# Reordering the opening of an FFT-plus-SoLU kernel: the zeroing of a table, a load of indices, and two small weight products

## The chip, the cores and the metric

The kernel runs on one core of one Trainium2 chip. Its time is the device time of one execution in microseconds (us). Before the change three runs gave 1119.38, 1119.64 and 1119.69 us, a median of 1119.64 us. The profile is one execution with the hardware profiler on.

The engines go by short names: PE is TensorE (its weight loads are PEld), DVE is VectorE, ACT is ScalarE, POOL is GpSimd, and SP is SyncE, which here only issues transfers. Lines are numbered as in the kernel before; L644 is its line 644.

## The reference

```
x: (8, 3136, 256)      w_in: (256, 1024)   w_out: (1024, 256)   g_ln: (1024)
X   = real(fft over axis 1, then fft over axis 2)          # the mixing block
x   = X.reshape(25088, 256)
h   = x @ w_in
sm  = softmax(h, axis=-1)
s   = h * sm                                                # SoLU
ln  = (s - mean(s)) / sqrt(var(s) + 1e-6) * g_ln
out = ln @ w_out
```

In this setup w_in and w_out are 64-bit floats in memory and are narrowed to 32 bits by integer and float operations on DVE and ACT.

## The kernel before, in words

The transform over the sequence (3136 = 49 x 64) is done in two steps, for pairs of batches (four pairs). Step one, `transform1`, multiplies slabs of x by the table F. Step two, `transform2`, multiplies the stored result by the table T. The transform over the features is not done on the data: it is folded into w_in once, at the start. `product_in(h, parts)` multiplies the cosine table Q into w_in and gives the folded matrix Wi, one half h of 128 rows at a time. Each half h has four parts: parts 0 and 2 read the upper half of w_in (c = 0), parts 1 and 3 the lower half (c = 1); parts 0 and 1 make the left 512 columns, parts 2 and 3 the right 512. `keep_in` copies the finished half from PSUM to Wi on ACT.

After the opening the kernel goes through 100 units of 128 or 256 rows each. In each, PE makes the rows' second transform and the up product, DVE and ACT make the softmax and the statistics, and PE makes the down product. The change does not touch this loop.

The order of instructions on each engine is written out by hand (`with tc.manual_schedule()`), so an engine executes in the order of the source, and a waiting instruction holds everything behind it on the same engine. The opening, which the change rearranges, consists of these pieces:

- **Loads.** SP issues, in order: the row indices `idx` (L806), the four pieces of w_in (`raw_in`, L591, 512 KB each), Q (L674), F (L818), and then the slabs of x. A slab c of the first pair (c = 0 to 7, four positions each) has two operands: `xa` or one half of `room`, read straight by SP (L128), and `xb` or the other half of `room`, its mirror image, gathered by POOL with an indirect DMA that needs `idx` (L130). The first six slabs are asked for at once, the last two when slabs 0 and 1 have been used. `gain` is g_ln in 8 rows of 128 (L678).
- **Narrowing of w_in**, piece by piece (0, 1: upper half left and right; 2, 3: lower half left and right). `exponent_in` takes the exponent bits (L594, DVE) and has ACT scale them in three steps (`confine`, L618, L620, L622). `narrow_in` then takes the mantissa (L594, then L635, its part 0), joins sign and exponent (L638, part 1, waits for ACT), and multiplies (L644, part 2).
- **Products.** `busy` runs four matmuls whose result is not used (L703). Then `product_in` (L698): before the change parts 0 and 2 of both halves, then parts 1 and 3 of half 0; parts 1 and 3 of half 1 come only behind slab 4.
- **First transform.** For each slab DVE adds the mirror image (`add_mirror`, L146, L148). Slabs 0 and 2 then go to PE directly (L214, four matmuls for each two positions); the others are first folded on DVE (`fold`, L153, L154, L166) into one of two `y` buffers and need two matmuls for each two positions (L225). ACT copies each result out (L228), and SP stores it to `zd` in DRAM (L233). Four PSUM banks are used in turn.
- **The norm weights.** `scale_out` transposes `gain` on PE (L722) into the PSUM bank that slab 3 uses next, and ACT scales it into `g_ln` (L723), which the narrowing of w_out needs. It stands behind slab 2.
- **The table T.** POOL zeroes it (two memsets, L829) behind the six gathers; SP fills its two diagonal blocks later (L683).
- **The end of the opening.** w_out is loaded after slab 3's turn (L717) and narrowed on DVE; `zd` is read back (L241), the second transform of the first units starts, and DVE meets the first unit at L302.

Of the kernel before, what the change touches and what calls it, by code (L numbers as in the profile page):

```python
# [45 lines left out]
def kernel(  # L46
# [19 lines left out]
    nc = tc.nc  # L66
# [3 lines left out]
    KD = D // P  # L70
# [21 lines left out]
    T = [const.tile([P, 2, n, N2], FP32, name=f"T{n}") for n in (KG, NK - KG)]  # L92
# [6 lines left out]
    idx = const.tile([P, NP * (NC + NK)], I32, name="idx")  # L99
# [19 lines left out]
    def load(pr, c, room=None):  # L119

        r = slice(pr.p * PR, (pr.p + 1) * PR)
        rows = PR if pr.p else P
        if room is None:
            xa = xpool.tile([P, CH, D], FP32, tag="xa", name="xa")
            xb = xpool.tile([P, CH, D], FP32, tag="xb", name="xb")
        else:
            xa, xb = (t.rearrange("p (l d) -> p l d", d=D) for t in room)
        nc.sync.dma_start(out=xa[0:rows], in_=x_pn[r.start : r.start + rows, c * CH + 1 : (c + 1) * CH + 1, :])  # L128
        i = pr.p * NC + c
        nc.gpsimd.indirect_dma_start(  # L130
            out=xb[0:rows].rearrange("p l d -> p (l d)"), out_offset=None, in_=x_g,
            in_offset=bass.IndirectOffsetOnAxis(ap=idx[0:rows, i : i + 1], axis=0))
        xa, xb = xa[0:PR], xb[0:PR]
        x0 = None
        if c == NC - 1:
            x0 = xpool.tile([PR, 1, D], FP32, tag="x0", name="x0", bufs=1)
            nc.sync.dma_start(out=x0, in_=x_pn[r, 0:1, :])
        pr.raw[c] = (xa, xb, x0)

    def add_mirror(pr, c, engine, part=None):  # L140

        xa, xb, _ = pr.raw[c]
        rows = (0, CH) if part is None else (part * CH // 2, (part + 1) * CH // 2)
        r = slice(rows[0], min(rows[1], CH - 1 if c == NC - 1 else CH))
        a, rb = xa[:, r, :], xb[:, ::-1, :][:, r, :]
        i = engine.tensor_tensor(out=a[:, :, 1:D], in0=a[:, :, 1:D], in1=rb[:, :, D - 1 : 0 : -1], op=ALU.add)  # L146
        if part is None:
            engine.tensor_tensor(out=a[:, :, 0:1], in0=a[:, :, 0:1], in1=rb[:, :, 0:1], op=ALU.add)  # L148
        return i
# [6 lines left out]
    def fold(pr, c):  # L156

        xa, _, x0 = pr.raw.pop(c)
        pr.y[c] = xpool.tile([PR, CH, D], FP32, tag="y", name="y")
        sides = [(pr.y[c], xa)]  # L160
        if c == NC - 1:
            pr.y0 = xpool.tile([PR, 1, D], FP32, tag="y0", name="y0", bufs=1)
            sides.append((pr.y0, x0))
        for o, i in sides:
            fold_features(o, i)
            nc.vector.tensor_copy(out=o[:, :, 0:129:128], in_=i[:, :, 0:129:128])  # L166
# [426 lines left out]
    def bits(o, i, a, op0, b=None, op1=ALU.bypass):  # L593
        nc.vector.tensor_scalar(out=o, in0=i, scalar1=a, scalar2=b, op0=op0, op1=op1)  # L594
# [11 lines left out]
    def confine(unit, here=False, parts=(0, 1, 2)):  # L606

        if unit is None:
            return
        if here:  # L610
            bits(unit, unit, -896.0, ALU.add, 0.0, ALU.max)
            bits(unit, unit, 255.0, ALU.min, 2.0 ** 23, ALU.mult)
            return

        u = unit.bitcast(FP32)
        for i in parts:
            if i == 0:
                nc.scalar.activation(out=u, in_=unit, func=ACT.Relu, bias=limits[:, 0:1])  # L618
            elif i == 1:
                nc.scalar.activation(out=u, in_=u, func=ACT.Relu, bias=limits[:, 1:2], scale=-1.0)  # L620
            else:
                nc.scalar.activation(out=unit, in_=u, func=ACT.Identity, bias=limits[:, 2:3], scale=-(2.0 ** 23))  # L622

    def narrow(w, raw, outs, unit, parts=range(3)):

        if w.dtype == FP32:
            if 2 in parts:
                for o, scale in outs:
                    nc.vector.tensor_scalar(out=o, in0=o, scalar1=scale, scalar2=2.0 ** 20, op0=ALU.mult, op1=ALU.mult)
            return  # L630
        lo, hi = raw[:, 0 : 2 * NW : 2], raw[:, 1 : 2 * NW : 2]
        m = lo.bitcast(FP32)
        if 0 in parts:
            bits(mantissa, hi, 0xFFFFF, ALU.bitwise_and, 0x100000, ALU.bitwise_or)
            nc.vector.scalar_tensor_tensor(out=m, in0=lo.bitcast(U32), scalar=2.0 ** -32, in1=mantissa, op0=ALU.mult,  # L635
                                           op1=ALU.add)
        if 1 in parts:
            nc.vector.scalar_tensor_tensor(out=unit, in0=hi, scalar=top_bit, in1=unit, op0=ALU.bitwise_and,  # L638
                                           op1=ALU.bitwise_or)
        if 2 in parts:  # L640
            n = NW // len(outs)
            for i, (o, scale) in enumerate(outs):
                r = slice(i * n, (i + 1) * n)
                nc.vector.scalar_tensor_tensor(out=o, in0=m[:, r], scalar=scale, in1=unit[:, r].bitcast(FP32),  # L644
                                               op0=ALU.mult, op1=ALU.mult)

    class Weights:
# [17 lines left out]
            self.units.append(exponent(w, raw))  # L665
            confine(self.units[-1])

        def narrow_in(self, i):
            w, raw, o, c, j, n = self.pieces[i]
            narrow(w, raw, [(o[:, j : j + n], 2.0 ** -19)], self.units.pop(0))  # L670

        def load_tables(self):
            self.Q = fpool.tile([P, KD, D + 1], FP32, tag="ev", name="Q", bufs=1)
# [129 lines left out]
    with tc.manual_schedule():  # L803
        pairs = [Pair(p) for p in range(NP)]
        first, weights = pairs[0], Weights()
        nc.sync.dma_start(out=idx, in_=mirror)  # L806
        make_identity(nc, ident)

        rooms = {}
        for c in range(2, 6, 2):  # L810
# [4 lines left out]
        for c in range(4):  # L815
            weights.piece_in(c)
        weights.load_tables()
        nc.sync.dma_start(out=F, in_=f_tab)  # L818
        for c in range(6):
            load(first, c, rooms.get(c))  # L820
            if c == 0:
                weights.load_gain()
        nc.vector.memset(ones, 1.0)
        nc.vector.memset(neg_half, -0.5)
        bits(top_bit, neg_half[:, 0:1].bitcast(I32), 31, ALU.logical_shift_right, 31, ALU.logical_shift_left)
        for i, limit in enumerate((-896.0, 255.0, 255.0 * 2.0 ** 23, 1e-12)):
            nc.vector.memset(limits[:, i : i + 1], limit)
        for t in T:
            nc.gpsimd.memset(t, 0.0)  # L829
        weights.exponent_in(0)  # L830
        for c in range(3):
            weights.exponent_in(c + 1)
            weights.narrow_in(c)
        weights.narrow_in(3)
        weights.mid()
        first.minus = fpool.tile([P, D], FP32, tag="ot1", name="minus", bufs=3)[0:PR, 0:ZR]
        nc.scalar.mul(out=first.minus, in_=F[:, 1, :], mul=-1.0)
        weights.busy(3, 4)
        made = [weights.product_in(h, (0, 2)) for h in range(KD)]
        weights.keep_in(0, weights.product_in(0, (1, 3), made[0]))  # L840
        for c in range(NC):

            add_mirror(first, c, nc.vector)
            if c not in BY_PE:
                fold(first, c)
            if c == NC - 1:
                for i in range(2):
                    weights.exponent_out(i)
                confine(weights.units[0], True)
                weights.narrow_out(0)  # L850
            if c == 3:
                weights.place_out()
                for i in range(2):
                    weights.load_out(i)
                weights.load_table(0)
                weights.scale_out()
            for s in range(CH // 2):
                if c == NC - 1:
                    confine(weights.units[0], parts=(s,))
                transform1(first, c * CH // 2 + s)  # L860
            first.raw.pop(c, None)
            if c + 6 < NC:
                load(first, c + 6)
            if c == 4:
                weights.keep_in(1, weights.product_in(1, (1, 3), made[1]))

        turn(first, 0, nc.sync, 0, 2)
        turn(first, 0, nc.gpsimd, 2, KG)
# [131 lines left out]
        for i in range(whole + 1, len(units) + lag + 1):  # L1000
# [84 lines left out]
            if i in (len(units), len(units) + 1):  # L1085
                w = i - len(units)
# [89 lines left out]
```

## Time and profile before

| what | value |
|---|---|
| median of three runs | 1119.64 us |
| the profiled execution's own time | 1119.93 us |
| its span, first to last instruction | 1117.8 us |
| PE busy | 1095.0 us (98%) |
| DVE busy | 976.6 us (87%) |
| ACT busy | 798.9 us (71%) |
| POOL busy | 809.2 us (72%) |
| first unit met by DVE (L302) | 52.76 us from the span's start |

The span leaves out 2.1 us that the execution's own time has around it. In a timeline line the first number is the start in us from the span's start, the second the time from the first to the last of the x instructions that the line merges, and a bracket at its end gives the idle time of that engine just before and what ended it. A name with "q" (SPq, POOLq) is the queue in which an engine issues transfers. In the forty slices a digit is the busy share of a slice of 27.9 us in tenths.

### The profile page before, as it was taken

What the parts mean: (1) busy time and instruction counts of PE and PEld (TensorE: products, weight loads), DVE (VectorE), ACT (ScalarE), POOL (GpSimd) and SP (SyncE); (2) the same over time, 40 slices, a digit from 0 to 9 for tenths busy, and PEclk for the clock granted to TensorE, in tenths of its full rate; (3) what the DMA queues carried; (4) which work ended last, traced back from release to release, by engine and by line L of the source; (5) the groups of instructions that cost most, each with busy time, mean ns of one, the idle gap of its engine ahead of it and who ended that gap; (6) DMA issues with size and microseconds to landing.
All of it is one profiled execution on the core that took longest, in us unless ns stands there. A gap on an engine that the chain in (4) does not pass through costs nothing. (4 is left out here: it accounts for less than half of the span.)

```text
span 1117.8 us, 22047 instructions
## 1 busy us (share of the span) xinstructions
PE 1095.0 (98%) x7055; PEld 875.5 (78%) x7055; DVE 976.6 (87%) x1432; ACT 798.9 (71%) x1947; POOL 809.2 (72%) x709
## 2 busy tenths in 40 slices
PE   5999999999999999999999999999999999999998
PEld 3557787878877878787788788787887788778888
DVE  7999888888888988889889989898898898998884
ACT  4598777777766777777766777777776777777771
POOL 4077888857867979775876878885775676866674
PEclk9999999999999999999999999999999999999999
DMA  9565887766978989766897888776696685865665
GB/s 347 195 186 123 180 205 181 177 144 142 181 175 171 198 180 199 178 147 141 154 182 171 189 184 196 183 176 149 138 165 141 138 172 114 164 140 114 141 133 125
DMA packets 457930, 187.75 MB, mean 168 GB/s; under 512 B 424646, under 2 KB 439254, under 8 KB 457816
## 3 DMA queue, kind: packets, MB, share of 16 engines
q1 hardware_dynamic: 443800, 146.94, 61.9%
q0 software_dynamic: 14016, 39.40, 13.1%
q8 instruction: 57, 0.93, 0.3%
q14 instruction: 57, 0.47, 0.1%
HBM read 46.75 MB, written 38.80 MB: 77 GB/s over the span
## 5 line engine op out<-in xcount | busy, mean ns | idle before, releaser
L289 PE MATMUL ps_h<-Wi,q 128*128 128x512 f32 x800 | 361.6, 593 | 0.3 <-DVE nmax L310 0.2
L465 POOL TENSOR_TENSOR S<-uT 128x512 f32<-128x512 f32 x186 | 237.5, 1277 | 107.6 <-DVE u L325 29.4
L472 PE MATMUL ps_m<-Ws,S 128*128 128x128 f32 x2304 | 296.0, 275 | 0.1
L472 PEld LDWEIGHTS ps_m<-Ws,S 128*128 128x128 f32 x2304 | 279.5, 192 | 3.2 <-issue 0.2
L332 ACT ACTIVATE h<-u,usum 128x1024 f32<-128x1024 f32 x196 | 224.9, 1148 | 71.5 <-DVE u L325 71.5
L289 PEld LDWEIGHTS ps_h<-Wi,q 128*128 128x128 f32 x800 | 144.2, 190 | 144.9 <-issue 141.9
L325 DVE SCALAR_TENSOR_TENSOR u<-h,u 128x1024 f32<-128x1024 f32 x196 | 232.8, 1223 | 11.0 <-ACT u L318 10.9
L318 ACT ACTIVATE u<-h,nmax 128x1024 f32<-128x1024 f32 x196 | 223.2, 1141 | 2.3 <-DVE nmax L310 1.1
L396 DVE STREAM_TRANSPOSE v<-u 128x2048 f32<-128x2048 f32 x88 | 203.4, 2311 | 3.0
L472 PE MATMUL ps_m<-Wo,uT 128*128 128x128 f32 x1536 | 203.7, 276 | 0.4 <-DMA out_dram<-ot 0.4
L472 PEld LDWEIGHTS ps_m<-Wo,uT 128*128 128x128 f32 x1536 | 187.9, 192 | 1.5 <-issue 1.5
L310 DVE CUSTOM_DVE_ANT_0 h<-ev,ps_h 128x1024 f32<-128x1024 f32 x100 | 122.1, 1221 | 17.1 <-DVE ev L302 9.3
L559 POOL DMA_INDIRECT out_dram<-ot,idx x96 | 110.5, 1151 | 29.0 <-issue 12.4
L310 DVE CUSTOM_DVE_ANT_0 h<-h,ps_h 128x1024 f32<-128x1024 f32 x96 | 117.2, 1221 | 14.2 <-ACT ot L516 0.5
L465 POOL TENSOR_TENSOR S<-uT,S 128x512 f32<-128x512 f32 x93 | 118.9, 1278 | 7.2
L465 POOL TENSOR_TENSOR S<-S,uT 128x512 f32<-128x512 f32 x93 | 118.8, 1277 | 7.3
L302 DVE SCALAR_TENSOR_TENSOR ev<-w_mid,r,ps_h 128x1024 f32<-128x1024 f32 x99 | 122.8, 1241 | 0.2
L472 PE MATMUL ps_m<-Ws,uT 128*128 128x128 f32 x768 | 101.8, 276 | 0.0
L472 PE MATMUL ps_m<-Wo,S 128*128 128x128 f32 x768 | 101.4, 275 | 0.0
L253 PEld LDWEIGHTS ps_m<-T,g 128*128 128x128 f32 x400 | 60.0, 191 | 47.9 <-issue 46.6
L507 ACT ACTIVATE ot<-ps_m,rs 128x256 f32<-128x256 f32 x96 | 45.5, 474 | 70.4 <-PE ps_m L472 50.4
L472 PEld LDWEIGHTS ps_m<-Ws,uT 128*128 128x128 f32 x768 | 93.8, 192 | 0.0
(122 smaller groups left out, 1213.9 us busy)
## 6 DMA issues: line engine op xcount, KB each, us to landing
uT<-v SPq DMA_DIRECT2D x752, 128.0 KB
g<-zd POOLq DMA_DIRECT2D x72, 160.0 KB, 5.2
out_dram<-ot SPq DMA_DIRECT2D x176, 64.0 KB
zd<-z SPq DMA_DIRECT2D x24, 400.0 KB
xa<-in_x_dram SPq DMA_DIRECT2D x24, 392.0 KB
raw_in<-in_moe_w_in_dram SPq DMA_DIRECT2D x4, 512.0 KB
xa<-in_x_dram SPq DMA_DIRECT2D x4, 512.0 KB
room<-in_x_dram SPq DMA_DIRECT2D x4, 512.0 KB
```

The costliest lines, as they stand in the source:

```text
L253: nc.tensor.matmul(o, g[:, k, h * P : (h + 1) * P], table, start=(h == 0), stop=True, skip_group_check=True)
L289: nc.tensor.matmul(ps[:, fs], t.q[:, c * P : (c + 1) * P], Wi[:, c, fs], start=True, stop=not whole_even)
L302: nc.vector.scalar_tensor_tensor(out=t.ev, in0=w_mid, scalar=t.r, in1=ps, op0=ALU.mult, op1=ALU.add)
L310: nc.vector.tensor_tensor_reduce(out=t.h[s], in0=t.h[0] if s else t.ev, in1=t.odd, scale=1.0 if s else -0.5, scalar=3.0e38, op0=ALU.add, o ...
L318: nc.scalar.activation(out=t.u[s], in_=t.h[s], func=ACT.Exp, bias=t.nmax[:, s : s + 1], scale=-1.0, accum_out=t.esum[:, s : s + 1])
L325: t.last = nc.vector.scalar_tensor_tensor(out=t.u[s], in0=t.h[s], scalar=-1.0, in1=t.u[s], op0=ALU.mult, op1=ALU.mult, accum_out=t.usum[:, ...
L332: nc.scalar.activation(out=t.h[s], in_=t.u[s], func=ACT.Square, bias=t.usum[:, s : s + 1], scale=-float(FF), accum_out=t.ssq[:, s : s + 1])
L396: nc.vector.transpose(out=t.batch.v[:, :, t.w], in_=t.both.rearrange("p s (g n) -> p (s g) n", n=32))
L465: i = engine.tensor_tensor(out=S[j], in0=a, in1=b, op=op)
L472: nc.tensor.matmul(o, a[:, c], b[:, c], start=start and c == 0, stop=c == n - 1, skip_group_check=True)
L507: nc.scalar.mul(out=self.t.ot[1], in_=self.PP, mul=self.rs[1])
L559: dma = nc.gpsimd.indirect_dma_start(out=out, out_offset=bass.IndirectOffsetOnAxis(ap=idx[:, i : i + 1], axis=0), in_=t.ot[s], in_offset=None)
```

## The change

Six things move; no computation of the loop is added or removed.

1. POOL zeroes T right after the identity matrix, ahead of the gathers.
2. The load of `idx` moves behind Q in SP's order. All six gathers on POOL wait for it.
3. The load of `gain` moves ahead of the slabs of x.
4. `narrow_in` is split: part 0 of piece c (mantissa) comes ahead of the exponent of piece c+1, parts 1 and 2 behind it.
5. `scale_out` (L722, L723) moves from behind slab 2 to the middle of the weight products.
6. Parts 1 and 3 of both halves are made ahead of the first transform, in the order part 1 of both, part 3 of both; both copies to Wi follow there. The product that stood behind slab 4 is gone from that place.

```diff
-        def narrow_in(self, i):
+        def narrow_in(self, i, parts):
             w, raw, o, c, j, n = self.pieces[i]
-            narrow(w, raw, [(o[:, j : j + n], 2.0 ** -19)], self.units.pop(0))
+            narrow(w, raw, [(o[:, j : j + n], 2.0 ** -19)], self.units.pop(0) if 2 in parts else self.units[0], parts)
...
-        nc.sync.dma_start(out=idx, in_=mirror)
         make_identity(nc, ident)
+        for t in T:
+            nc.gpsimd.memset(t, 0.0)
...
         weights.load_tables()
+        nc.sync.dma_start(out=idx, in_=mirror)
         nc.sync.dma_start(out=F, in_=f_tab)
+        weights.load_gain()
         for c in range(6):
             load(first, c, rooms.get(c))
-            if c == 0:
-                weights.load_gain()
...
-        for t in T:
-            nc.gpsimd.memset(t, 0.0)
         weights.exponent_in(0)
-        for c in range(3):
-            weights.exponent_in(c + 1)
-            weights.narrow_in(c)
-        weights.narrow_in(3)
+        for c in range(4):
+            weights.narrow_in(c, (0,))
+            if c < 3:
+                weights.exponent_in(c + 1)
+            weights.narrow_in(c, (1, 2))
...
         made = [weights.product_in(h, (0, 2)) for h in range(KD)]
-        weights.keep_in(0, weights.product_in(0, (1, 3), made[0]))
+        weights.scale_out()
+        for part in (1, 3):
+            for h in range(KD):
+                weights.product_in(h, (part,), made[h])
+        for h in range(KD):
+            weights.keep_in(h, made[h])
...
                 weights.load_table(0)
-                weights.scale_out()
...
-            if c == 4:
-                weights.keep_in(1, weights.product_in(1, (1, 3), made[1]))
```

## The prediction

> **What bounds the kernel now.** I read the busy shares first, then the slices, then the opening as timelines by engine. PE is busy for 98% of the span and is the bound of the 100 units; only the first slice is loose.
>
> ```profile
> PE 1095.0 (98%) x7055; PEld 875.5 (78%) x7055; DVE 976.6 (87%) x1432; ACT 798.9 (71%) x1947; POOL 809.2 (72%) x709
> ...
> PE   5999999999999999999999999999999999999998
> ...
> DVE  7999888888888988889889989898898898998884
> ```
>
> So whatever the change is worth is worth in the first 53 us. Every later unit hangs on the one before, so I take a shift at the first L302 (52.76 us) to reach the end whole. In the opening DVE is the engine without gaps. Its timeline, and POOL's, between 8 and 16 us:
>
> ```profile
> 9.50 0.69 DVE L644 SCALAR_TENSOR_TENSOR w_in<-raw_in,S 128x512 f32<-128x512 f32 x1
> 10.11 3.61 DVE L594 TENSOR_SCALAR S<-raw_in 128x512 int32<-128x512 int32 x2
> 13.74 0.69 DVE L635 SCALAR_TENSOR_TENSOR raw_in<-raw_in,S 128x512 f32<-128x512 uint32 x1
> ```
> ```profile
> 10.26 2.84 POOL L829 MEMSET T<- 128x640 f32 x2
> ```
> ```profile
> L594 DVE TENSOR_SCALAR S<-raw_in x8: 406/427/3279, 5.8 to 18.5; 128x512 int32<-128x512 int32 x8
> ```
>
> The last line gives shortest, median and longest in ns: one of eight equal instructions takes 3279 instead of 427, and it lies exactly over POOL's zeroing of T. That is a stall of 2.85 us inside an instruction, which no list of waits shows.
>
> From 22.34 us on PE takes over as the bound of the opening:
>
> ```profile
> 10.33 3.60 PE L703 MATMUL ps_m<-w_in,ident 128*128 128x256 f32 x8 [10.33 <-DVE w_in L644]
> 15.09 4.72 PE L698 MATMUL wps<-w_in,Q 128*128 128x512 f32 x10 [1.16 <-DMA Q<-in_q_tab_dram]
> 21.14 1.13 PE L698 MATMUL wps<-w_in,Q 128*128 128x512 f32 x2 [1.32 <-DVE w_in L644]
> 22.34 1.54 PE L214 MATMUL ps_m<-xa,F 98*100 98x258 f32 x6
> ...
> 31.12 0.22 PE L722 MATMUL ps_m<-ident,gain 8*128 8x8 f32 x1
> 31.95 3.70 PE L225 MATMUL ps_m<-y,F 98*100 98x258 f32 x16 [0.60 <-ACT g_ln L723]
> 35.48 1.88 PE L698 MATMUL wps<-w_in,Q 128*128 128x512 f32 x4
> ```
>
> DVE then waits for PE to free a `y` buffer (1.59 us ahead of L153 at 33.96, 0.28 at 39.13).
>
> [...] 3279 - 427 = 2852 ns against a zeroing of 2.84 us. [...] eight passes of 128x256 take 3.60 us at 10.33 (0.45 each), four take 1.03 at 46.32 (0.26 each[...]). [...] gathers and direct loads share about 0.41 MB/us from 8 to 28 us, and the gathers of slabs 2 to 5, all issued by 10.3, land at 15.8, 18.3, 20.9 and 23.5, one in 2.55 us.
>
> **The change part by part.** Old times are the trace's; new ones are my estimates from its durations.
>
> *Zeroing first.* 2.84 us on POOL from 1.3 to 4.2. It lies behind no gather, since `idx` is not there yet, and over DVE's small memsets at 0.83 to 1.5, which may wait for it; what hides that is the first w_in piece. If that landed ahead of 4.2, the cover would be gone. DVE gains 2.85.
>
> *`idx` behind Q.* SP's first w_in issue goes from 1.18 to 0.73 (-0.45). The 66 KB of `idx` (0.25 us) and the first gather no longer share with piece 0 (another 0.2). Piece 0 landed at 5.77 (DVE's first L594); I take 4.85, bounds 4.4 and 5.6. In exchange all six gathers wait. Pieces 0 to 3 landed at 5.76, 7.02, 9.21 and 11.59, Q at 15.07 (SP's issues at those times wait for them), with gathers taking some 1.0 of 3.2 MB by 11.6. Without them piece 3 lands near 8.5, Q near 9.9, `idx` near 10.4 (bounds 9.2 and 12.5).
>
> *Narrowing order.* A piece costs DVE 2.79 (15.74 to 18.53), the last one 2.47 (18.53 to 21.00). The first now runs exponent, mantissa, L635, next exponent, and waits for ACT, whose chain ended 2.69 after the first exponent began (5.77 to 8.46): L638 at +2.75, L644 over at +4.14 (before, 10.11 - 5.77 = 4.34 with one piece's exponent waited for). End at 4.14 + 2 x 2.79 + 2.47 = 12.2 after the landing: 17.05 instead of 21.00, so DVE is 3.95 ahead. By instruction the split itself is worth only some 0.2.
>
> *Products and gain.* PE can start `busy` when L644 of piece 0 is over, at 9.2 (before 10.33): 3.6 us, to 12.8. Each L698 is two passes 0.427 apart (16.49, 16.92, 17.35): parts 0 and 2 of both halves are 8 passes, to 16.2; L722 with its switch 0.3, to 16.5; part 1 twice 1.7, to 18.2; part 3 twice 1.7, to 19.95. Piece 3 is ready at 17.1 and slab 0's mirror sum at 18.35, so both are early: **PE is late next**, and slab 0 starts at 19.95 instead of 22.34 (-2.4). [...] `busy` now runs straight into the products, [...] 0 to 1.6 us. I take 0.5.
> ACT's second copy to Wi (1.01) ends near 21.2, and slab 0's first result comes at 21.7: hidden. Behind it waits L228, then SP's stores.
>
> *Bubble at slab 3.* With `scale_out` gone, PE goes from slab 2 to 3 without 30.98 to 31.95, as DVE folded slab 3 at 28.6. Slab 3 starts at 19.95 + 8.64 = 28.6 (old 31.95: -3.35).
>
> *Products behind slab 4.* 1.7 us of PE leave (35.27 to 36.98), but are not all won: slab 5's fold starts when slab 3 is over (+2.01: 30.6), and from there DVE's chain sets the pace, fold 1.3, mirror sum 1.3, fold 1.3, mirror sum 1.0, fold 1.3 and the last row 0.5. PE needs 1.73 per slab and waits for slabs 6 and 7. Only the 0.28 wait at 39.13 goes. DVE reaches w_out (40.88) at 37.25: -3.63. PE's last slab moves as much, and so do the store, the reading back of `zd` (a chain of issue and landing that keeps its length), and L302.
>
> *Gathers.* With `idx` at 10.4 the first gather lands near 15.6, the rest 2.55 apart at most: 18.2, 20.7, 23.3, 25.8, 28.4 (earlier once SP's own slabs are in). PE's times ask for 18.6, 20.6, 23.7, 25.9, 27.6 and 29.3: hidden, by 0.9 us (slab 5) to 3.0.
> w_out is asked for 2.4 earlier and needed 3.6 earlier; its first half landed some 3 us ahead of use. Hidden.
>
> **Sum.** DVE -3.95; waits for slab 3 +0.6; wait at 39.13 -0.28: -3.63. [...] +0.5: -3.1. The profiled execution's own time, 1119.93, becomes 1116.8. It stands 0.29 above the median of the runs shown, so the forecast is 1119.64 - 3.1 = 1116.5.
>
> **The rivals.** A change of 0.2%, 2.2 us, is about what a measurement of this kernel can tell from none.
>
> *A: as above* (72%), 1115.0 to 1117.4 by the bounds of piece 0 (-0.45, +0.75) and [...] (-0.5, +1.1).
>
> *B: the gathers come just too late* (12%). `idx` lands at 12.5 or a little after. For: it lies in order behind 2.4 MB, and Q alone took 3.5 us to land (11.59 to 15.07). Against: that was with the gathers in between. At 12.9 slab 5 lands at 30.9, 1.6 late, and the gain falls from 3.1 to 1.5: about 1118.1.
>
> *C: [...] piece 0 hardly earlier* (9%). 1.6 instead of 0.5, and 5.6 instead of 4.85: -3.1 + 1.1 + 0.75: about 1118.4. That the change doesn't shorten the stall belongs here: if DVE's last tiny memsets met a still running zeroing beyond 4.85, the same size.
>
> *D: slower* (5%). The place is POOL's first L130. If Q still lands at 15 and `idx` at 17.5, and gathers keep 2.55 each, slab 5 lands at 17.5 + 1.15 + 1.4 + 6 x 2.55 = 35.4; its mirror sum was at 31.08 and had until 32.7 before (33.96 less 1.29). 2.7 late, less the 0.28 at 39.13: +2.4, 1122.0. It decides from `idx` at about 15 on; with the direct slabs in by then, gathers should go faster than 2.55, which speaks against it.
>
> *E: more than A* (2%): [...] piece 0 at 4.4, PE as early as data allow: 1115.0 or less.
>
> **How the numbers follow.** The likeliest is A, 1116.5. The range 1115.0 to 1118.2 leaves out E, D and most of C. Faster by over 0.2% (under 1117.4): nearly all of A, a little of B, and E: 0.80. Within 0.2%: B, C and A's edge: 0.15. Slower: 0.05.
>
> **What would show it.** In the profile after: no L594 above 0.5 us among the w_in pieces; POOL's memsets over by 4.5; its first gather at 9 to 12.5; DVE's first mirror sum at 16.5 to 17.8; PE's first L214 19.9 to 21, directly behind L698; no gap at slab 3; L302 near 49.6. It is wrong if L146 or PE waits for a gather, if the first pieces land at 5.7 as before, or if L302 is early and the span is not.

## The result, and the profile after

The change makes the kernel a little faster: a median of 1117.45 us over 22 runs against 1119.39 us over 22 runs of the kernel before on the same chips, a ratio of 0.9983 (95% interval 0.9976 to 0.9990), 1.9 us. The forecast of 1116.5 meant 3.1; the measured time lies inside the range of 1115.0 to 1118.2. The profiled execution took 1118.62 us with a span of 1116.8.

The stall is gone. The groups of one tile (w_in's raw pieces), with shortest, median and longest in ns, after the change:

```profile
L594 DVE TENSOR_SCALAR S<-raw_in x8: 420/425/596, 4.3 to 14.1; 128x512 int32<-128x512 int32 x8
```

The longest is 596 instead of 3279, and that one (12.25 to 12.85) begins while POOL issues its first gather (11.30 to 12.62). POOL's timeline shows where the zeroing went, and what came of the gathers:

```profile
1.26 2.80 POOL L808 MEMSET T<- 128x640 f32 x2
11.30 1.32 POOL L130 DMA_INDIRECT xb<-in_x_dram,idx  x1 [7.25 <-DMA idx<-in_mirror_dram]
12.92 1.42 POOL L130 DMA_INDIRECT xb<-in_x_dram,idx  x1 [0.30 <-issue]
```

The zeroing is over at 4.06 and POOL then sits idle for 7.25 us, waiting for `idx`, with all six gathers behind that wait. DVE's timeline shows who pays. Before:

```profile
20.39 0.69 DVE L644 SCALAR_TENSOR_TENSOR w_in<-raw_in,S 128x512 f32<-128x512 f32 x1
21.00 1.21 DVE L146 TENSOR_TENSOR xa<-xa,xb 98x1020 f32<-98x1020 f32 x1
...
22.22 1.22 DVE L146 TENSOR_TENSOR xa<-xa,xb 98x1020 f32<-98x1020 f32 x1
...
33.96 0.69 DVE L153 TENSOR_TENSOR y<-room 98x508 f32<-98x508 f32 x1 [1.59 <-PE ps_m L225]
...
39.13 0.69 DVE L153 TENSOR_TENSOR y<-xa 98x508 f32<-98x508 f32 x1 [0.28 <-PE ps_m L225]
...
40.88 0.75 DVE L594 TENSOR_SCALAR S<-raw_out 128x512 int32<-128x512 int32 x2
...
52.76 1.28 DVE L302 SCALAR_TENSOR_TENSOR ev<-w_mid,r,ps_h 128x1024 f32<-128x1024 f32 x1
```

After:

```profile
16.06 0.69 DVE L644 SCALAR_TENSOR_TENSOR w_in<-raw_in,S 128x512 f32<-128x512 f32 x1
19.35 1.22 DVE L146 TENSOR_TENSOR xa<-xa,xb 98x1020 f32<-98x1020 f32 x1 [2.60 <-DMA xb<-in_x_dram,idx]
...
21.92 1.22 DVE L146 TENSOR_TENSOR xa<-xa,xb 98x1020 f32<-98x1020 f32 x1 [1.27 <-DMA xb<-in_x_dram,idx]
...
32.10 0.69 DVE L153 TENSOR_TENSOR y<-room 98x508 f32<-98x508 f32 x1
...
38.77 0.75 DVE L594 TENSOR_SCALAR S<-raw_out 128x512 int32<-128x512 int32 x2
...
51.00 1.28 DVE L302 SCALAR_TENSOR_TENSOR ev<-w_mid,r,ps_h 128x1024 f32<-128x1024 f32 x1 [0.25 <-PE ps_h L289]
```

The narrowing ends at 16.75 (16.06 + 0.69) instead of 21.08, 4.33 earlier, more than the 3.95 of the forecast. DVE then waits 2.60 us for the first gather and 1.27 for the second, so slab 1's mirror sum starts at 21.92 instead of 22.22: 0.30 is left. From there on DVE has no stop until w_out; the waits for PE of 1.59 and 0.28 are gone, and that is where the gain of this execution comes from: 0.30 + 1.87 = 2.17, and DVE reaches w_out (L594) at 38.77 instead of 40.88 (-2.11). A little of that is lost again at L302, which now waits 0.25 for PE. PE's side:

```profile
8.62 3.75 PE L703 MATMUL ps_m<-w_in,ident 128*128 128x256 f32 x8 [8.62 <-DVE w_in L644]
12.17 3.83 PE L698 MATMUL wps<-w_in,Q 128*128 128x512 f32 x8
15.92 0.22 PE L722 MATMUL ps_m<-ident,gain 8*128 8x8 f32 x1
16.07 3.70 PE L698 MATMUL wps<-w_in,Q 128*128 128x512 f32 x8
20.71 1.54 PE L214 MATMUL ps_m<-xa,F 98*100 98x258 f32 x6 [0.93 <-DVE xa L148]
```

PE is through with the products near 19.8, as the forecast had it, and then waits 0.93 us: in this execution not PE is late next, but the gathers.

L302 moved by 1.76. The shift does reach the end: the L302 at 1026.17 before stands at 1024.49 after (-1.68). In the last 12 us 0.6 more goes, as PE waits for a store of `ot` (0.38 before, 0.99 after, 1.22 in a second profile of the same kernel, nothing in the profiles of e_hold, e_zero_only and v_hold3_small), so the span of this one execution shrinks by 1.0 only.

### The profile page after: what moved, and what is told of

Read it like the earlier page. It is cut to its first block, busy times and chain, and to the rows that moved or that the text cites. A ratio compares the mean times of both kernels' runs of the same rounds, so it can differ in the third digit from the quotient of the medians.

```text
span 1116.8 us, 22049 instructions
## 1 busy us (share of the span) xinstructions
PE 1095.4 (98%) x7055; PEld 875.8 (78%) x7055; DVE 974.5 (87%) x1432; ACT 799.0 (72%) x1947; POOL 809.5 (72%) x709
## 5 line engine op out<-in xcount | busy, mean ns | idle before, releaser
L302 DVE SCALAR_TENSOR_TENSOR ev<-w_mid,r,ps_h 128x1024 f32<-128x1024 f32 x99 | 122.9, 1241 | 0.5 <-PE ps_h L289 0.2
```

Of the source, the lines that this page charges most:

```text
L302: nc.vector.scalar_tensor_tensor(out=t.ev, in0=w_mid, scalar=t.r, in1=ps, op0=ALU.mult, op1=ALU.add)
```

## The experiments

All were compared with the kernel before on the same chip; ratios carry a 95% interval. The finer reading is the time of the first L302 in each profile, though it turns out to move by a microsecond between two profiles of one kernel. Theory 1: the late gathers eat what the narrowing gains. Theory 2: PE's row of products is the limit.

### The zeroing alone

```diff
# the kernel before, with
         make_identity(nc, ident)
+        for t in T:
+            nc.gpsimd.memset(t, 0.0)
```

> The kernel before with edit 1 alone (T zeroed first). Theory 1: no L594 over 0.6 us, narrowing over near 18.1 instead of 21.00, no wait for xb; PE's four first products wait for Q until 15, then run through, slab 0 starts near 20.2, the bubble at slab 3 stays; L302 near 50.6, a gain of 2.1 us, as much as the whole change brings. Rival (the stall of 2.85 us was covered by something else, Q or the slabs): L302 at 52.3 or later, a gain under 0.5 us.

Measured: ratio 0.9982 (0.9972 to 0.9992).

```profile
L594 DVE TENSOR_SCALAR S<-raw_in x8: 418/420/429, 5.8 to 15.5; 128x512 int32<-128x512 int32 x8
```

No L594 takes over 0.43 us, the narrowing is over at 17.93, slab 0 on PE at 19.66, bubble in place, L302 at 51.02. The whole change had 0.9983 and 51.00. So one moved pair of memsets is worth all that the six edits were measured to bring. It does one thing more than end the stall: the gathers start behind the zeroing, at 4.23 instead of 2.86, and PE no longer waits for Q (1.16 before). It fell short of 50.6 since slab 1's direct load came at 20.69, after a wait of 1.47 us, and slab 3's after another 0.94:

```profile
20.69 1.22 DVE L146 TENSOR_TENSOR xa<-xa,xb 98x1020 f32<-98x1020 f32 x1 [1.47 <-DMA xa<-in_x_dram]
```

### Products and gain alone

```diff
# the kernel before, with
-        weights.keep_in(0, weights.product_in(0, (1, 3), made[0]))
+        weights.scale_out()
+        for part in (1, 3):
+            for h in range(KD):
+                weights.product_in(h, (part,), made[h])
+        for h in range(KD):
+            weights.keep_in(h, made[h])
...
-                weights.scale_out()
...
-            if c == 4:
-                weights.keep_in(1, weights.product_in(1, (1, 3), made[1]))
```

> The kernel before with edits 5 and 6 alone (norm weights and all products ahead of the first transform). The stall of DVE stays, narrowing over at 21.0, part 3 of both halves only then: slab 0 on PE at 22.9 instead of 22.34; no bubble at slab 3, whose fold wait on DVE shrinks. If the moves are worth what the accounting of the traces says (1.86 for the wait for slab 3, 0.28 for the other, less 0.6 for the later start of slab 0): L302 near 51.8, some 1.0 earlier. If PE's later start cancels them: 52.5 to 53.

Measured: ratio 1.0007 (0.9999 to 1.0015), no gain; L302 at 52.17. In this execution the zeroing happened to start ahead of the instruction that it blocked, and blocked it for less. DVE's timeline, then POOL's:

```profile
12.13 2.21 DVE L594 TENSOR_SCALAR S<-raw_in 128x512 int32<-128x512 int32 x2
```
```profile
10.90 2.82 POOL L829 MEMSET T<- 128x640 f32 x2
```

The zeroing ends at 13.72; the longest of the eight took 1879 ns. By these two executions the size of the stall is a matter of when the two meet: 2.85 us where DVE's instruction began 0.15 us ahead of the memset, 1.45 (1879 ns less 427) where it began 1.2 us into it. It also makes this profile no clean test of the products, as the stall was 1.4 us shorter than before; that they gain nothing alone rests on the ratio. PE found a new wait here: 1.15 us for `gain` at L722, since in this kernel `gain` stands behind a slab of x. In the full change edit 3 takes care of that.

### The change without its second edit

```diff
# the changed kernel, with
+        nc.sync.dma_start(out=idx, in_=mirror)
         make_identity(nc, ident)
...
-        nc.sync.dma_start(out=idx, in_=mirror)
```

> The changed kernel with the load of idx back in first place (edit 2 undone, the rest kept). Theory 1 (the gathers start too late and eat what the narrowing gains): first gather near 4.1 us, right behind the zeroing of T, its data landed near 12, no wait for xb at L146; the narrowing over near 17.3. But Q has to share with the gathers again and lands near 14, so PE's products run to 21.3 and slab 0 starts there; L302 near 50.5 (51.00 in the changed kernel, 52.76 before). Theory 2 (PE's chain of products [...] is what limits, the gathers hardly matter): slab 0 starts at 20.7 as in the changed kernel and L302 stays at 51.0 or later.

Measured (this kernel is e_idx_first): ratio 0.9990 (0.9983 to 0.9997); L302 at 51.38. First gather at 4.23 and no wait for any gather, as theory 1 said. But piece 0 of w_in lands at 5.93 instead of 4.27, PE's eight first passes take from 13.85 to 18.4, and slab 0 starts at 22.01. PE does not wait for Q here, as theory 1 had it: it begins the products late because piece 0 was late, and the first eight passes are slow, 4.54 us where the next eight take 3.70. DVE waits 0.64 and 1.26 for the direct loads of slabs 1 and 3. So `idx` in first place is not shown to be better: what the gathers win, w_in and the direct loads lose. Neither theory alone holds. Gathers and direct loads are in the same 16 DMA engines (in each us from 14 to 18 POOL's queue took 48.5 to 53.4% of them and SP's 50.0 to 52.3%), and edit 2 moves the wait from the direct loads to the gathers.

### The change without its products

```diff
# the changed kernel, with
-        weights.scale_out()
-        for part in (1, 3):
...
+        weights.keep_in(0, weights.product_in(0, (1, 3), made[0]))
...
+                weights.scale_out()
...
+            if c == 4:
+                weights.keep_in(1, weights.product_in(1, (1, 3), made[1]))
```

> The changed kernel with the norm weights' transpose and the products of half 1 back in their old places (edits 5 and 6 undone). Theory 1 (DVE waits for the first two gathers until 19.35 and 21.92 whatever PE does; what the change wins comes after that, from PE's shorter row of work): slab 0 again at 20.7, the wait for slab 3 of 1.6 us on DVE is back, L302 near 52.5, nearly the whole gain lost. Theory 2 (PE late with the products): slab 0 starts earlier, near 19 to 20, and L302 is 51.3 or earlier.

Measured: ratio 0.9992 (0.9985 to 0.9999); L302 at 51.44. Slab 0 starts at 20.44, again set by the first gather (mirror sum at 19.09 after 2.27 of waiting), so having the products ahead of it cost the changed kernel nothing in its first profile. The waits for PE are back, 0.84 and 0.28. The loss against the changed kernel is 0.4 or 1.5 by its two profiles, less than the 1.5 of theory 1 by the first and as much by the second; the ratios, 0.9992 and 0.9983, have intervals that overlap, so the products' share is not settled.

### The changed kernel again

> The changed kernel once more, to see how much the opening moves from one execution to another. First gather at 11 to 11.5, DVE waits at the first two L146 for 3.5 to 4 us together, L302 at 50.7 to 51.5; the part of the span behind L302 1064.4 to 1065.8 us, as in the profiles so far.

Measured: ratio 0.9985 (0.9978 to 0.9991); L302 at 49.93, 1.07 earlier than in the first profile and outside what I expected. `idx` landed at 10.67, the first gather at 18.54 after a wait of 1.25, the second at 21.10 after 1.26: 2.5 together, where 3.5 to 4 were expected. PE's first eight passes took 4.33 here, so the products were over only at 20.5, 0.6 behind slab 0's mirror sum; both lines of work were late at once. One profile therefore fixes L302 to a microsecond only. The part behind it was 1065.9, 0.1 above my band, by the wait for the store.

### Why the first gather takes eight microseconds

```diff
# the changed kernel, with
-        for c in range(6):
+        for c in range(2):
             load(first, c, rooms.get(c))
...
             weights.narrow_in(c, (1, 2))
+            if c == 2:
+                for i in range(2, 6):
+                    nc.vector.memset(rooms[i][0][:, 0:1], 0.0)
+                    load(first, i, rooms[i])
```

> The changed kernel, with SP's direct loads of slabs 2 to 5 held back until piece 2 of w_in is narrowed (a one-column memset by DVE in each of the four tiles just ahead of the load; four tiny DVE instructions more). It tells apart why the first gather took 8 us from its issue at 11.30 to 19.35. Sharing with the direct loads: with the queue of SP nearly empty from 12 to 14, the gather's bytes flow from about 12.5 and xb of slab 0 lands by 16.5; no wait at the first L146. A delay of some 4.6 us between the issue of a gather and its first byte, whatever else moves: first bytes at 15.9 as in the changed kernel, landing near 17.5 since it shares less then; DVE still waits about 0.8 us. In both, slabs 2 to 5 may come late instead.

Measured (e_hold): ratio 0.9987 (0.9981 to 0.9994); L302 at 50.41, no wait at the first L146, 2.07 at the second. The DMA queues by stretch, packets, MB and share of the 16 engines, tell why; q0 is POOL's queue, q1 is SP's. The changed kernel from 11 to 15 us, its first gather having been issued at 11.30, and from 15 to 17:

```profile
q1 hardware_dynamic: 416, 1.51, 101.3%
```
```profile
q1 hardware_dynamic: 159, 0.57, 72.0%
q0 software_dynamic: 62, 0.25, 31.6%
```

And with the direct loads held, first gather issued at 11.42, from 13 to 15 us:

```profile
q0 software_dynamic: 101, 0.41, 69.3%
q1 hardware_dynamic: 56, 0.17, 21.6%
```

In the changed kernel the gather moves no byte that shows for nearly four us while SP's queue fills the engines. With four direct loads less in that queue, bytes flow from 13.3: the first show 1.9 us after the issue instead of 4.5. So the row of direct loads counts for rather more than half of the delay (2.6 of 4.5 us), and neither reading alone is right. DVE narrows w_in through both delays alike (to 16.75 here, to 16.82 in e_hold), so its work is not what made the difference. The second gather then ran into the released loads.

```diff
# e_hold, with
-            if c == 2:
+            if c == 3:
```

> The changed kernel with SP's direct loads of slabs 2 to 5 held until piece 3 of w_in is narrowed (16 us; e_hold held them until piece 2, 14 us, and the second gather then stood still from 17 us on). Theory: what makes the first two gathers late is the row of direct loads ahead of them in the DMA engines. Then the gathers of slabs 0 and 1 land by 16 and 17.5, no wait at the first two L146, DVE goes on from the narrowing (16.5) without a stop until slab 2's direct load, which lands near 19 to 20.5; slab 0 on PE near 20 to 20.7 behind the products, L302 near 49.5. Rival (a delay from issue to first byte of 4.6 us, whatever else moves): wait of 1 us or more at the first L146, L302 50.4 or later, as in e_hold.

Measured (v_hold3): ratio 0.9996 (0.9988 to 1.0004); L302 at 51.03. The first gather moves its first bytes 2.3 us after its issue (11.24, 13.52). Both first mirror sums start without a wait, at 16.98 and 18.23, as the theory said; slab 2's direct load, asked for at 17.08, then stops DVE for 3.17 us, which the theory had not. The bytes were late in another order.

### Other orders of the loads

```diff
# the changed kernel, with
-        for c in range(4):
-            weights.piece_in(c)
-        weights.load_tables()
-        nc.sync.dma_start(out=idx, in_=mirror)
+        weights.piece_in(0)
+        nc.sync.dma_start(out=idx[:, 0:NC], in_=mirror[:, 0:NC])
+        weights.piece_in(1)
+        weights.load_tables()
+        for c in range(2, 4):
+            weights.piece_in(c)
         nc.sync.dma_start(out=F, in_=f_tab)
         weights.load_gain()
+        nc.sync.dma_start(out=idx[:, NC:], in_=mirror[:, NC:])
```

> The changed kernel with another order of SP's loads: piece 0 of w_in, the eight columns of idx that the first pair needs (4 KB instead of 66 KB), piece 1, Q, pieces 2 and 3, F, gain, the rest of idx. The gathers start behind the zeroing at 4.2, Q lands near 9 to 10. Theory 1 (gathers behind Q cost what the narrowing gains): narrowing over near 16.5, no or a short wait at L146 (slab 1's direct load may be late, as it is when the gathers go first: up to 20.3), slab 0 on PE near 19.6, L302 near 49.5, 1.5 earlier than in the changed kernel, 3.3 earlier than before. Theory 2 (PE's chain or DVE's chain limits): L302 not under 50.5.

Measured (v_small_idx): L302 at 50.16 in the profile, which was the fastest of all its executions (1116.66); ratio 0.9993 (0.9985 to 1.0001). Slab 0 reached PE at 19.51. DVE waited for direct loads, 1.25 for slab 1 and 1.26 for slab 3.

```diff
# v_small_idx, with
-        weights.piece_in(1)
-        weights.load_tables()
-        for c in range(2, 4):
+        for c in range(1, 4):
             weights.piece_in(c)
+        weights.load_tables()
+        nc.sync.dma_start(out=idx[:, NC:], in_=mirror[:, NC:])
...
-        nc.sync.dma_start(out=idx[:, NC:], in_=mirror[:, NC:])
```

> As v_small_idx, but Q stays behind all four pieces of w_in. It tells what Q's place is worth once the gathers start early: Q has to share with them and lands near 13 to 14, the products end later: slab 0 on PE near 21.3, L302 near 50.5 to 51. If Q's place does not matter, the same as v_small_idx within 0.3.

Measured (e_small_idx_q_late): L302 at 51.06, slab 0 at 21.14, both numbers as forecast, but a late Q is the smaller part of it: PE waited 0.48 us for Q, and its first eight passes then took 4.55 instead of 3.60, while DVE waited 2.65 and 1.25 for the direct loads of slabs 0 and 1. The timed runs are slower than that profile: a ratio of 1.0013 (1.0004 to 1.0021) and a median of 1120.63, where the profiled execution, with 1117.63 the fastest of fourteen, is at the edge of a spread that reaches 1123.60. By their medians v_small_idx and this kernel run 1.9 and 3.0 us slower than their profiled executions; e_idx_first, whose gathers are as early, does not (1118.46 profiled, 1118.15 the median).

```diff
# v_small_idx, with
-        for c in range(6):
+        for c in range(2):
...
+            if c == 1:
+                for i in range(2, 6):
+                    nc.vector.memset(rooms[i][0][:, 0:1], 0.0)
+                    nc.vector.memset(rooms[i][1][:, 0:1], 0.0)
+                    load(first, i, rooms[i])
```

> The changed kernel with v_small_idx's order of SP's loads (piece 0, eight columns of idx, piece 1, Q, pieces 2, 3), and both loads of slabs 2 to 5, direct and gathered, held until piece 1 of w_in is narrowed (11 us), so that slabs 0 and 1 have the DMA engines ahead of the rest. Theory (order of the bytes decides): no wait at the first two L146 (17.3 and 18.5), slab 0 on PE at 19.5, L302 near 49.0 to 49.5, the best of all. Rival (PE's and DVE's own chains limit by then): L302 50 or later though the waits are gone.

Measured (v_two_first): ratio 0.9980 (0.9972 to 0.9989), but L302 at 51.23: DVE waited 0.77, 1.26 and 1.26 for direct loads of slabs 0, 1 and 3. The expectation of no waits was wrong.

```diff
# v_hold3, with
-        for c in range(4):
+        for c in range(3):
             weights.piece_in(c)
+        nc.sync.dma_start(out=idx[:, 0:NC], in_=mirror[:, 0:NC])
+        weights.piece_in(3)
         weights.load_tables()
-        nc.sync.dma_start(out=idx, in_=mirror)
...
+        nc.sync.dma_start(out=idx[:, NC:], in_=mirror[:, NC:])
```

> v_hold3 with the eight columns of idx that the first pair needs ahead of piece 3 of w_in, the rest behind gain. The gathers start near 9 instead of 11.3, with only piece 3, Q, F and two direct loads beside them: Q lands near 11.5 to 12.5, xb of slabs 0 and 1 by 14 and 16, no wait for them; L302 as in v_hold3 or up to 0.5 earlier. If the early gathers hold up Q beyond 12.5, slab 0 on PE is late by as much and L302 is later than in v_hold3.

Measured (v_hold3_small): ratio 0.9979 (0.9972 to 0.9986), L302 at 49.76. The first gather, issued at 8.34, still moved nothing until 12.66, as piece 3, Q, F and two slabs stood in SP's queue, which took 95 to 115% of the engines in each us from 7 to 13. Then, with that queue almost empty, the gathers took the engines nearly alone, from 13 to 15 us:

```profile
q0 software_dynamic: 208, 0.79, 98.2%
q1 hardware_dynamic: 21, 0.04, 5.0%
```

That is 0.40 MB/us, twice the 0.2 that I had carried over. Slab 2's direct load then cost DVE a wait of 2.39 us.

```diff
# v_hold3_small, with
-        for c in range(2):
+        for c in range(3):
...
-                for i in range(2, 6):
+                for i in range(3, 6):
```

> v_hold3_small with slab 2's direct load not held (only slabs 3 to 5 wait for piece 3). In v_hold3_small DVE waited 2.39 us for that load at the third L146. Theory: it lands by 17 to 18 now, at the price of up to 0.5 us on the first gathers; no wait at the first three L146, about 1 us at slab 3; DVE is then ahead of PE until slab 3 is over, L302 near 49.2 (49.76 in v_hold3_small). Rival (the gathers fall behind the third direct load as in the changed kernel): first L146 waits 1 us or more, L302 50 or later.

Measured: ratio 0.9979 (0.9972 to 0.9987), a median of 1117.00; L302 at 49.91. No wait at the first three mirror sums, 1.85 at slab 3, and 0.68 for PE ahead of slab 5's fold. The forecast L302 of 49.2 was missed by 0.7: PE's products were over only at 20.4, as its first eight passes took 4.57 us. Both last versions have slightly lower medians than the changed kernel (1117.27 and 1117.00 against 1117.45); the intervals of their ratios overlap almost whole, so nothing here is shown to beat it.

## Why the prediction was right or wrong

The direction and the range held, and so did the chain up to the end of the narrowing; behind it the mechanism did not. By the prediction's own sign ("It is wrong if L146 or PE waits for a gather") it failed, as L146 waited 3.87 us. DVE was forecast to reach w_out 3.63 earlier and came 2.11 earlier: the narrowing gave 4.33 instead of 3.95, the gathers took 3.87 where nothing was put down, and the wait for slab 3, forecast to grow by 0.6, vanished with its whole 1.59, because DVE itself came late. That a loss in one term removed a wait in another is what kept the number in the range; the forecast had not seen it. By its own steps:

- **Zeroing first**: right. 2.80 us, over at 4.06, and the cover held by a hair, as piece 0 was met at 4.27. Alone it brings what the whole change brings. That its full 2.85 are a matter of meeting was not seen: the stall was 1.45 in the kernel with the products alone. By the recorded starts DVE's instruction came 0.15 us ahead of the memset and was the one held. What in the chip holds it, no run shows.
- **Piece 0 and narrowing order**: right in kind. Piece 0 at 4.27 (forecast 4.85, and earlier than the bound of 4.4), narrowing over at 16.75 (17.05), so it took 12.5 from the landing (12.2), with the ACT wait of 0.87 at the first L638.
- **Products**: PE ready near 19.8 (forecast 19.95 before the 0.5 taken on top). That 0.5, and its bounds of 0 and 1.6, were the author's estimate for products that run slower at first; the profile before showed slow passes in `busy` (128x256 in 0.45 us each at 10.33, against 0.26 at 46.32). The first eight passes took 3.60 to 4.68 in kernels whose products follow `busy` at once, the next eight 3.70 in each of those that have them, so the term came out as 0 to 1.0. The cause was not shown: the granted clock reads 1.00 in every 2 us of the first 50 of the profile after, whose first eight took 3.83. The term cost this execution nothing, since PE waited for the slab anyway.
- **Gathers, "hidden, by 0.9 to 3.0": this is the step that failed.** `idx` came at 11.3 instead of 10.4, inside the bounds. But the first gather landed at 19.35, 8.05 us after its issue, where the sum had 5.2. The term left out was the time to its first byte: 1.15 for issuing, as the profile before has it, and about 1.4 to the data, an estimate that no profile shows, 2.55 together. The sum is about what e_hold and v_hold3 show behind a short queue (1.9 and 2.3), but behind SP's row of loads 4.5 us passed from the issue to the first byte (11.30 to 15.85). In the profile after, the two queues shared the engines only once the gather had begun to move, where the prediction had them do so from the start: SP's 101.3% and no byte of POOL's from 11 to 15 us, then 48.6% and 58.2% from 16 to 17. The kernel before had shown that delay already: its first gather, issued at 2.86, moved nothing until 7.58. From 3 to 7 us q0 does not appear at all.

```profile
q1 hardware_dynamic: 322, 1.19, 94.2%
```

  I took its landing 8.9 us after issue for a sharing of bandwidth with w_in, and carried over only the later pitch of 2.55 us.
- **"PE is late next"**: wrong for that reason in the first profile; in the second PE was late as well, by 0.6. The later slabs were hidden, as forecast: no wait for a gather from slab 2 on.
- **Bubble, products behind slab 4, waits for PE**: the bubble went and so did both waits, though not for the reason given: with the zeroing alone the bubble and the products stayed in their old places, and DVE did not wait for PE either.
- **Rivals**: B had the kind of mechanism (gathers just too late), at the wrong threshold and the wrong slab: it put the turn at an `idx` of 12.5 and at slab 5; 11.3 was enough, and slabs 0 and 1 were late. It gave 1118.1; the measured 1117.45 lies between it and A. A's own range does not follow from its bounds: -0.45 - 0.5 and +0.75 + 1.1 around 1116.5 give 1115.6 to 1118.4, so C is A's upper end, and E's sum gives 1115.6 too.

What the runs show of the balance is that the terms do not add. The zeroing alone gives 0.9982, the products alone nothing, the change without the products 0.9992, and the whole 0.9983, each known to about 0.001. The changed kernel's first 20 us are full of loads (DMA share 0.95 to 1.06 in every 2 us from 4 to 20), and each order tried left some slab late: the mirror image of slab 0, 1 or 3, or the direct load of slab 0, 1, 2 or 3.

What stays open: why most runs of v_small_idx and e_small_idx_q_late are 2 to 3 us slower than their profiled executions; what sets the delay behind a full queue, which was 4.2 to 5.0 us in the other twelve profiles, whether the gather was issued at 2.9 or at 11.3; and what edits 2, 3 and 4 are worth, as none was run alone. With profiles of one kernel a microsecond apart, differences of L302 under that are no evidence by themselves; this holds for most of those between the kernels above.

## What to carry to other kernels

The stall inside an instruction showed nowhere but in a longest duration far above the median of equal instructions (3279 ns against 427); look there, and lay the other engines' timelines over it. Before a load is moved behind others, count the bytes ahead of it and measure from issue to first byte, not only the pitch of the landings. SP's queue filled the engines here (101.3% from 11 to 15 us), and moving `idx` was a trade with the loads that it passed: in first place it spared DVE 3.87 us of waiting for gathers and brought piece 0 at 5.93 instead of 4.27. So price the loser too.

## What the runs showed of the hardware

- POOL's memset held DVE's `tensor_scalar` (128x512, int32) in both orders of recorded start: 3279 ns instead of 427 where DVE's instruction began 0.15 us ahead of the memset, 1879 ns where it began 1.2 us into it. Both times DVE's instruction ended 0.29 us after the memset did (13.39 and 13.10; 14.01 and 13.72). The memset itself was not lengthened: 2.84 and 2.82 us, and 2.80 with DVE idle.
- A gather being issued by POOL seems to hold the same instruction too, but far less. Over the fourteen profiles, of the L594 on w_in's pieces that met no memset, 17 took over 450 ns (up to 652), and all 17 lay over the issue of a gather; 43 others lay over one and were not lengthened, and none of the 50 that met no gather was.
- A gather by POOL moved no byte for over four us while SP's queue filled the 16 engines (94.2% from 3 to 7 us before, 101.3% from 11 to 15 after; before: issued 2.86, first bytes at 7.58; after: issued 11.30, first bytes at 15.85), against 1.9 and 2.3 us with that queue short (e_hold, v_hold3), and the gathers ran at 0.40 MB/us when they had the engines nearly alone (v_hold3_small, 98.2% of them from 13 to 15 us).
